# Softmax sums in four 64 x 64 matmuls instead of eight 128 x 32, and a smaller scratch for software DMA

## The chip, the cores and the metric

The kernel runs on one core of a Trainium2 chip. The metric is the device time of one execution in microseconds; lower is better. Of the kernel before, three runs were timed: 1777.71, 1780.35 and 1787.36 us, median 1780.35. One more execution was recorded by the hardware profiler; all durations below are from it.

The core has five engines, each with its own queue of instructions: PE (TensorE, matmuls, and PEld for its weight loads), DVE (VectorE), ACT (ScalarE), POOL (GpSimd) and SP (SyncE, here only a queue that issues DMAs). Sixteen DMA engines move data. A DMA that SP or ACT issues is described by hardware; one that POOL issues is described by software, in a scratch space in SBUF whose size the kernel sets.

## What is computed

`x` has 2048 rows of 1024. The result is `x + A(LN(x)) + B(LN(x))`. B is a dense layer, a tanh-GELU and a dense layer (1024 to 3584 to 1024). A is attention with a recurrent memory: the sequence is cut into 64 segments of 32 rows; each segment attends to itself and to 8 memory rows, and the first 8 rows of its output are the next segment's memory:

```python
mem = mem0                                     # 8 rows
for s in range(n_seg):                         # 64 segments, one after the other
    h = concatenate([mem, xs], axis=1)         # 8 + 32 rows
    q, k, v = h @ Wq, h @ Wk, h @ Wv           # 32 heads of 128
    scores = where(mask, q @ k.T * scale, -1e9)
    p = softmax(scores)
    o = (p @ v) @ Wo
    mem = o[:, :8]
    outs.append(o[:, 8:])
```

Each of the four weights has 1024 x 4096 bf16 values, 8 MB. Together they are 32 MB, more than SBUF holds, so a part has to come from HBM again in each segment.

## The kernel before

It works in two stages. The first (0 to about 400 us) is the layer norm and B, for all rows; its result, with `x` added, goes to HBM as the residual (`res_d`, `resL_d`), and the normalized rows go there turned, ready to be weights (`rows_d`, `rowsL_d`).

The second stage is a loop over the 64 segments, written out in full by Python. A segment has eight half passes (K, Q, V and O, each in halves u = 0 and 1 of 16 heads), and each half pass has eight weight units of 128 x 2048 values (512 KB). In the first six the 32 rows of the segment are the stationary operand, loaded into the array as 128 x 32 column tiles, and the weights stream past: `product` (L830) makes four matmuls of 512 columns for a unit, in the four column tiles of the array, which run side by side. `o_product` (L1089) does the same with the attention's output. Of the 64 units, 47 stay in SBUF and 17 are streamed, 15 of them by SP's DMAs from HBM into a ring of six slots (L284) and two from copies that are kept in PSUM (L273, DVE). A slot is filled again once PE has used it.

Order is written out by hand (`manual_schedule`): steps of the attention are put between the units of a half pass by tables such as `SUMS_0`, `SUMS_1`, `VALUES_0`. For one half u the steps are: `scores` (L947, L953: PE, results in the PSUM bank `mixed`), `exps` (ACT, then a mask by DVE), `sums` (below), and `values` (L1039, L1045: PE, tiles of 64 rows x 128 columns, into two other banks). `sums` occurs 128 times: twice a segment.

In `sums` the exponentials of a half lie on the partitions as four blocks of 32, one for each residue j of the head number; `prA` has 4 x 40 columns, `prB` 4 x 2 x 8. For each block j, a matmul against a column of ones (and zeros elsewhere, `bd[:, j:j+1]`, spread over 32 columns) puts the sum over the block's partitions on all 32 partitions of that block: four matmuls for `prA` (L985, 160 columns) and four for `prB` (L991, 64 columns, added to the same place). ACT turns the sums into reciprocals by Ln and Exp (L996, L999); the Exp is done twice, with a bias `off` that blanks every other head, and DVE multiplies (L1012, L1017, L1024).

Between two segments the first rows of the output go back as memory: DVE adds (L1221), `put_mem` (L320) turns them by a matmul with `ident_mem`, four runs of 8 columns of the identity, and DVE copies them (L330) into `hr_home`, beside the rows of `x` for the next segment. After that, DVE adds the residual to the output (L1243), which PE's next half pass does not need, but which stands on DVE's queue ahead of the K turn (L896, L913) that it does need.

From segment 7 on POOL's queue has, for each segment (`loads`; before that ACT's queue):

- the output of the last segment, four copies of 12 KB (L1276); where i4 = s mod 4 is 1 at the segment that ended, two copies to `outL_d` (L1249) and five from there to the output (L1273) instead
- the next segment's rows, 64 KB (L292), into the half of `hr_home` that the output leaves
- if i4 = 0, `hrL` for the rows that four segments share, 64 KB (L297)
- this segment's residual, 64 KB (L1182), once PE has done with the rows there; if i4 = 1, `resL` too, 64 KB (L1208)
- if i4 = 3, a copy in SBUF (L1191)

In segments 1 to 4 POOL also copies the last residuals within HBM (L523).

The low end of SBUF is laid out by hand: at byte 0 of each partition the scratch for software DMA (`SCRATCH`, 320 bytes), behind it `hr_home`, `qL`, `pd_main` and `ident_mem`, then three slots `low0` to `low2`, up to byte 16384.

Of the kernel before, what the change touches and what calls it, by code (L numbers as in the profile page):

```python
# [10 lines left out]
BF16 = mybir.dt.bfloat16  # L11
U32 = mybir.dt.uint32
F32 = mybir.dt.float32
# [4 lines left out]
P = 128  # L18
# [20 lines left out]
NL = SEG - NX  # L39
# [6 lines left out]
NUNIT = 64  # L46
STREAMED = 17
LOW = 3
SCRATCH = 320
SMALL = 3776  # L50
LEAD = 6
AHEAD = 2
ADD_FIRST = 4
# [67 lines left out]
def kernel(  # L121
# [16 lines left out]
    nc = tc.nc  # L138
# [25 lines left out]
    place = nc.lookup_mloc("DynamicDMAScratchLoc")  # L164
    assert place.addr == 0 and list(place.dims) == [P, SCRATCH + SMALL + LOW * 4096]
    nc.dynamic_dma_scratch_size = SCRATCH
    place.dims = [P, SCRATCH]
    nc.lookup_mls("DynamicDMAScratchLoc").tensor_shape = [P, SCRATCH]
    low = {
        f"low{k}": nc.alloc_sbuf_tensor_at(f"low{k}", [P, 2048], BF16, offset=SCRATCH + SMALL + 4096 * k) for k in range(LOW)  # L170
    }

    hr_home = nc.alloc_sbuf_tensor_at("hr_home", [P, 512], BF16, offset=SCRATCH)[:, :]
    qL = [
# [7 lines left out]

    homes = [hr_home[:, 0:256], hr_home[:, 256:512]]
    small_consts = consts.tile([P, 16], BF16, name="small_consts")
    bd, off = small_consts[:, 0:4], small_consts[:, 4:8].bitcast(F32)

    def slab(place):
        if place in low:
# [3 lines left out]

    ident = homes[1][:, 0:P]
    make_identity(nc, ident)
    ident_mem = nc.alloc_sbuf_tensor_at("ident_mem", [P, 4, NL], BF16, offset=SCRATCH + 3712)[:, :, :]
    nc.vector.tensor_copy(out=ident_mem[:, :, :], in_=ident.rearrange("p (j t) -> p j t", j=4)[:, :, NX:SEG])
    nc.vector.memset(bd[:, :], 0.0)
    nc.vector.memset(off[:, :], NEVER)
    for j in range(4):
        q = slice(32 * j, 32 * j + 32)  # L200
        nc.vector.memset(bd[q, j:j + 1], 1.0)
        nc.vector.memset(off[q, j % 2:j % 2 + 1], 0.0)


# [144 lines left out]
    with tc.tile_pool(name="ma", bufs=2) as ma:  # L349
# [235 lines left out]
        for tg in range(4):  # L585
# [57 lines left out]
            if not last:  # L643
# [7 lines left out]
                for t in range(4):  # L651
# [6 lines left out]
                    for nb in range(2):  # L658
                        cs = slice(nb * 512, (nb + 1) * 512)
                        ps = new_ps()  # L660
                        for fc in range(FC):
                            nc.tensor.matmul(  # L662
                                ps[:, :],
                                lhsT=gts[fc // 4][:, fc % 4, t * P:(t + 1) * P],
                                rhs=w2_sb[fc // 2][:, fc % 2, cs],
                                start=(fc == 0),
                                stop=(fc == FC - 1),
# [68 lines left out]
    with tc.tile_pool(name="late", bufs=1) as late:  # L736
# [66 lines left out]
        for s in range(NSEG):  # L803
# [123 lines left out]
            def ends(t):  # L927

                return t.rearrange("p c (a b) -> p c a b", b=NL)[:, :, ::4, :]
# [50 lines left out]
            def sums(u):  # L980
                prA, prB = st["pr", u]
                dA = mixed[:, 0:160].rearrange("p (c q) -> p c q", q=40)
                for j in range(4):
                    q = slice(32 * j, 32 * j + 32)
                    nc.tensor.matmul(  # L985
                        dA[q, :, :], lhsT=bd[:, j:j + 1].to_broadcast([P, 32]), rhs=prA, start=True, stop=False,
                        skip_group_check=True, tile_position=(0, 32 * j),
                    )
                for j in range(4):
                    q = slice(32 * j, 32 * j + 32)  # L990
                    nc.tensor.matmul(  # L991
                        ends(dA[q, :, :]), lhsT=bd[:, j:j + 1].to_broadcast([P, 32]),
                        rhs=prB,
                        start=False, stop=True, skip_group_check=True, tile_position=(0, 32 * j),
                    )
                nc.scalar.activation(out=mixed[:, 0:160], in_=mixed[:, 0:160], func=ACT.Ln)  # L996

                for b in (1, 0):
                    nc.scalar.activation(  # L999
                        out=mixed[:, 160 * b:160 * b + 160], in_=mixed[:, 0:160], func=ACT.Exp, scale=-1.0,  # L1000
                        bias=off[:, b:b + 1],
                    )
                pdA = pd_main.rearrange("p (c b q) -> p c b q", c=4, b=2)
                if u:
                    pdB = q_all[:, 512:640].rearrange("p (c b a q) -> p c b a q", c=4, b=2, q=NL)
                else:
                    c0 = 0 if first else NL * slot
                    pdB = left_outs[1 if first or i4 >= 2 else 0][:, :, c0:c0 + NL].rearrange(
                        "p (c b a) q -> p c b a q", c=4, b=2
                    )  # L1010
                dd = mixed[:, 0:320].rearrange("p (b c q) -> p b c q", b=2, q=40)
                nc.vector.tensor_tensor(  # L1012
                    out=pdA.rearrange("p c b q -> p b c q"), in0=prA[:, None, :, :].to_broadcast([P, 2, 4, 40]),
                    in1=dd, op=ALU.mult,
                )
                if u:
                    nc.vector.tensor_tensor(  # L1017
                        out=pdB.rearrange("p c b a q -> p b c a q"),
                        in0=prB[:, None, :, :, :].to_broadcast([P, 2, 4, 2, NL]),
                        in1=dd.rearrange("p b c (e q) -> p b c e q", q=NL)[:, :, :, ::4, :], op=ALU.mult,  # L1020
                    )
                else:
                    for a in range(2):
                        nc.vector.tensor_tensor(  # L1024
                            out=pdB[:, :, :, a, :].rearrange("p c b q -> p b c q"),
                            in0=prB[:, None, :, a, :].to_broadcast([P, 2, 4, NL]),
                            in1=dd[:, :, :, 32 * a:32 * a + NL], op=ALU.mult,
                        )
                st["pd", u] = pdA, pdB
# [98 lines left out]
            if left_q[0] and not first:  # L1128
# [6 lines left out]
                0: [lambda: nc.vector.transpose(out=nat_home, in_=nat_home)],  # L1135
            }
            at[4 if first else SUMS_0[i4]] = [lambda: sums(0)] + ([] if first else [lambda: q_left(1)])
            if left_q[1] and not first:
                at[0].insert(0, lambda: keep_q(1))
# [29 lines left out]
            else:  # L1169
                at.setdefault(n0, []).append(lambda: values(0, (0,)))  # L1170
                at.setdefault(n1, []).append(lambda: values(0, (1,)))
            at.setdefault(5 if first else SUMS_1[i4], []).append(lambda: sums(1))

            psV1, psV1L = half_pass("V", 1, left_v[1], at)
# [139 lines left out]
```

## Time and profile before

| | us |
|---|---|
| runs, median (3) | 1780.35 (1777.71 to 1787.36) |
| the profiled execution | 1788.29 |
| its span, first to last instruction | 1786.6 |
| PE busy | 1697.1 (95%) |
| DVE, ACT, POOL busy | 987.9, 670.5, 300.4 |
| mean granted PE clock | 0.998 |
| HBM read, written | 573.43 MB, 28.90 MB |
| L985, first four matmuls of `sums` | x512, 33.2 busy |
| L991, second four | x512, 27.9 busy |

How to read it: a group of instructions is named by its line in the kernel, its engine and operation and its tiles (output, arrow, inputs). Matmuls in different column tiles overlap, so 512 L985 of about 235 ns each make only 33.2 us of busy time; what a step costs PE is read from the starts. A bracket in a timeline is the time that the engine stood idle before the instruction, and what ended it; "issue" there is idle time that nothing in the profile explains. The times "to landing" of a DMA run from its issue to the last byte's arrival.

### The profile page before, as it was taken

How to read it: one execution, taken by the hardware profiler on the slowest of the kernel's cores; microseconds unless marked ns; L12 is line 12 of the kernel's file. 1: busy time of each engine (PE TensorE's matmuls, PEld its weight loads, DVE VectorE, ACT ScalarE, POOL GpSimd, SP SyncE). 2: the span in 40 equal slices, each digit the busy share in tenths (PEclk: the TensorE clock that was granted, in tenths of full speed). 3: DMA queues.
4: the chain of work that ended last, by engine and by line, in shares of the span. 5: the costliest groups of instructions: out<-in, count | busy, mean ns of one | idle time of the engine just before them, and what ended most of it. 6: DMA issues, size and time to landing. Idle time of an engine off the chain costs nothing.

```text
span 1786.6 us, 70503 instructions
## 1 busy us (share of the span) xinstructions
PE 1697.1 (95%) x30600; PEld 867.5 (49%) x30600; DVE 987.9 (55%) x2642; ACT 670.5 (38%) x1709; POOL 300.4 (17%) x586
## 2 busy tenths in 40 slices
PE   9999999998999999999999999999999999999988
PEld 5444444444445544444545444454445445445444
DVE  7657483825555555555555555555555555555544
ACT  6334251603333333333333333343334333333333
POOL 0000002401231111111121211111121111111111
PEclk9999999999999999999999999999999999999999
DMA  9455312779999999999999999999999999999998
GB/s 278 146 167 169 91 45 71 267 277 335 387 390 388 387 374 383 380 383 367 393 378 382 374 381 393 389 388 389 375 387 400 389 389 394 380 378 396 378 376 316
DMA packets 232827, 594.37 MB, mean 333 GB/s; under 512 B 57715, under 2 KB 88035, under 8 KB 232516
## 3 DMA queue, kind: packets, MB, share of 16 engines
q1 hardware_dynamic: 197584, 567.08, 84.3%
q0 software_dynamic: 16896, 16.85, 2.8%
q10 hardware_dynamic: 18036, 5.94, 1.3%
q8 instruction: 239, 3.92, 0.9%
q14 instruction: 72, 0.59, 0.1%
HBM read 573.43 MB, written 28.90 MB: 337 GB/s over the span
## 4 chain that ended last, share of the span: by engine, by line
PE 70%; DMA 18%; DVE 4%; issue 3%; ACT 3%; ACTq 1%; SPq 1%; DVEq 0%
PE acc L830 36%; PE acc L1089 11%; PE ps L534 10%; DMA u<-Wc_O 10%; PE ps L662 6%; DMA u<-Wc_V 5%; PE ps L693 3%; PE acc L1039 1%; ACTq L459 1%; ACT mixed L999 1%; PE mixed L947 1%; SPq L521 1%; DMA hr_home<-res_d 1%; DVE pd_main L1012 1%; PE mixed L320 1%
## 5 line engine op out<-in xcount | busy, mean ns | idle before, releaser
L830 PE MATMUL acc<-u,hr_home 128*32 128x512 bf16 x11520 | 763.6, 380 | 19.7 <-DMA u<-Wc_V 10.2
L830 PEld LDWEIGHTS <-hr_home 128*32 128x32 bf16 x12288 | 337.8, 96 | 303.2 <-issue 45.2
L830 PE MATMUL acc<-u,hrL 128*32 128x512 bf16 x2880 | 253.0, 382 | 4.0 <-DMA hrL<-rowsL_d 2.1
L534 PE MATMUL ps<-u 128*128 128x512 bf16 (+1 forms) x992 | 195.1, 358 | 0.4 <-DMA u<-in_B_w_dram 0.4
L273 DVE TENSOR_SCALAR u<-kept 128x512 uint32<-128x512 uint32 x254 | 163.1, 684 | 48.0 <-PE acc L830 40.6
L1089 PE MATMUL acc<-u,d_oL 128*32 128x512 bf16 x2592 | 170.4, 380 | 13.0 <-issue 10.2
L882 ACT CAST d_oL<-acc 128x512 bf16<-128x512 f32 x143 | 82.0, 584 | 253.9 <-PE acc L830 220.9
L662 PE MATMUL ps<-u 128*128 128x512 bf16 x672 | 146.0, 379 | 0.0
L534 PEld LDWEIGHTS <-u 128*128 128x128 bf16 x992 | 91.6, 98 | 102.1 <-DMA u<-in_B_w_dram 0.6
L1089 PE MATMUL acc<-u,kq 128*32 128x512 bf16 (+1 forms) x2696 | 132.4, 320 | 8.1 <-DMA u<-Wc_O 6.4
L1012 DVE TENSOR_TENSOR pd_main<-kq,mixed 128x320 bf16<-128x320 bf16 x128 | 62.5, 488 | 129.2 <-ACT mixed L999 129.2
L909 ACT CAST kq<-acc 128x256 bf16<-128x256 f32 x256 | 89.4, 375 | 109.7 <-PE acc L830 76.6
L1089 PEld LDWEIGHTS <-kq 128*32 128x32 bf16 x3344 | 87.4, 96 | 84.0 <-ACT kq L1058 24.2
L1276 POOL DMA_DIRECT2D out_dram<-hr_home x168 | 85.4, 516 | 220.5 <-DVE hr_home L1243 220.5
L913 DVE STREAM_TRANSPOSE kq<-kq 128x256 bf16<-128x256 bf16 x256 | 98.2, 422 | 42.8 <-ACT kq L909 42.7
L886 ACT CAST kq<-acc 128x512 bf16<-128x512 f32 x128 | 75.2, 588 | 114.1 <-PE mixed L953 111.7
L977 DVE TENSOR_TENSOR kq<-kq,mixed 128x96 bf16<-128x96 bf16 (+1 forms) x256 | 38.1, 190 | 143.8 <-ACT kq L967 87.2
L830 PEld LDWEIGHTS <-hrL 128*32 128x32 bf16 x3072 | 86.3, 96 | 58.4 <-issue 3.7
L662 PEld LDWEIGHTS <-u 128*128 128x128 bf16 x672 | 65.5, 98 | 78.8 <-DVE u L619 0.4
L611 ACT ACTIVATE u<-ps,b1col 128x512 bf16<-128x512 f32 x112 | 76.5, 684 | 64.5 <-PE ps L534 61.7
L1089 PEld LDWEIGHTS <-d_oL 128*32 128x32 bf16 x2592 | 64.0, 96 | 69.5 <-issue 23.5
L999 ACT ACTIVATE mixed<-mixed,small_consts 128x160 f32<-128x160 f32 x256 | 94.2, 368 | 8.4
(127 smaller groups left out, 1910.5 us busy)
## 6 DMA issues: line engine op xcount, KB each, us to landing
u<-Wc_K SPq DMA_DIRECT2D x256, 512.0 KB
u<-Wc_V SPq DMA_DIRECT2D x256, 512.0 KB
u<-Wc_O SPq DMA_DIRECT2D x256, 512.0 KB
u<-Wc_Q SPq DMA_DIRECT2D x192, 512.0 KB
u<-in_B_w_dram SPq DMA_DIRECT2D x28, 512.0 KB
u<-in_A_Wq_dram SPq DMA_DIRECT2D x13, 512.0 KB
u<-in_A_Wv_dram SPq DMA_DIRECT2D x12, 512.0 KB
u<-in_A_Wk_dram SPq DMA_DIRECT2D x9, 512.0 KB
```

Of the source, the lines that this page charges most:

```text
L273: nc.vector.tensor_single_scalar(out=out, in_=in_, scalar=0, op=ALU.bitwise_or)
L534: nc.tensor.matmul(ps[:, SEG * s0:SEG * s1].rearrange("p (s t) -> p s t", t=SEG), lhsT=w1_sb[fb // 2][:, kt, (fb % 2) * P:(fb % 2 + 1) * P ...
L611: nc.scalar.activation(out=xb[:, :], in_=ps[:, :], func=ACT.Identity, bias=b1col[:, fb:fb + 1], scale=1.0)
L662: nc.tensor.matmul(ps[:, :], lhsT=gts[fc // 4][:, fc % 4, t * P:(t + 1) * P], rhs=w2_sb[fc // 2][:, fc % 2, cs], start=(fc == 0), stop=(fc ...
L830: nc.tensor.matmul(o, lhsT=lhs[:, i, :], rhs=m, start=(i == seq[0]), stop=(i == seq[-1]), tile_position=(0, 32 * j),)
L882: cp(out=out, in_=ps.rearrange("p (h e) -> p h e", e=32))
L909: nc.scalar.copy(out=q_home[:, h0:h1, NL:40], in_=ps[:, 32 * h0:32 * h1].rearrange("p (h e) -> p h e", e=32))
L913: nc.vector.transpose(out=half, in_=half)
L999: nc.scalar.activation(out=mixed[:, 160 * b:160 * b + 160], in_=mixed[:, 0:160], func=ACT.Exp, scale=-1.0, bias=off[:, b:b + 1],)
L1012: nc.vector.tensor_tensor(out=pdA.rearrange("p c b q -> p b c q"), in0=prA[:, None, :, :].to_broadcast([P, 2, 4, 40]), in1=dd, op=ALU.mult,)
L1089: nc.tensor.matmul(acc[r0:r0 + rows, 0:256 * len(blocks)], lhsT=lhsT, skip_group_check=True, rhs=o_columns(t, k, blocks), start=start, sto ...
L1276: loads.dma_start(out=out_flat[rows, 256 * j:256 * j + 256], in_=res[32 * j:32 * j + NX, :])
```

## The change

The ones are kept as `of_head`, 128 x 64: rows of even blocks have ones in columns 0 to 31, rows of odd blocks in columns 32 to 63. A matmul takes 64 partitions (two blocks) at once and gives 64 partitions of sums, so two matmuls do for `prA` and two for `prB`, in the tiles (0, 0) and (64, 64) of the array. `of_head` takes 128 bytes of a partition, where `ident_mem` had 64. To make room the scratch for software DMA shrinks from 320 to 256 bytes, everything between it and `low0` moves down by 64 bytes, and `ident_mem` goes to byte 16384, into unused bytes of the 32-byte cells of small constants, as four runs of 16 bytes, 32 bytes apart. `bd` is gone from `small_consts`.

```diff
-SCRATCH = 320
-SMALL = 3776
+SCRATCH = 256
+SMALL = 3840
...
-    bd, off = small_consts[:, 0:4], small_consts[:, 4:8].bitcast(F32)
+    off = small_consts[:, 0:4].bitcast(F32)
...
-    ident_mem = nc.alloc_sbuf_tensor_at("ident_mem", [P, 4, NL], BF16, offset=SCRATCH + 3712)[:, :, :]
+    ident_mem = nc.alloc_sbuf_tensor_at("ident_mem", [P, 4, 2 * NL], BF16, offset=16384)[:, :, 4:4 + NL]
+    of_head = nc.alloc_sbuf_tensor_at("of_head", [P, 64], BF16, offset=SCRATCH + 3712)[:, :]
...
-    nc.vector.memset(bd[:, :], 0.0)
+    nc.vector.memset(of_head[:, :], 0.0)
...
-        nc.vector.memset(bd[q, j:j + 1], 1.0)
+        nc.vector.memset(of_head[q, 32 * (j % 2):32 * (j % 2) + 32], 1.0)
...
-                for j in range(4):
-                    q = slice(32 * j, 32 * j + 32)
+                for r in range(2):
+                    q = slice(64 * r, 64 * r + 64)
                     nc.tensor.matmul(
-                        dA[q, :, :], lhsT=bd[:, j:j + 1].to_broadcast([P, 32]), rhs=prA, start=True, stop=False,
-                        skip_group_check=True, tile_position=(0, 32 * j),
+                        dA[q, :, :], lhsT=of_head[q, :], rhs=prA[q], start=True, stop=False,
+                        skip_group_check=True, tile_position=(64 * r, 64 * r),
                     )
-                for j in range(4):
-                    q = slice(32 * j, 32 * j + 32)
+                for r in range(2):
+                    q = slice(64 * r, 64 * r + 64)
                     nc.tensor.matmul(
-                        ends(dA[q, :, :]), lhsT=bd[:, j:j + 1].to_broadcast([P, 32]),
-                        rhs=prB,
-                        start=False, stop=True, skip_group_check=True, tile_position=(0, 32 * j),
+                        ends(dA[q, :, :]), lhsT=of_head[q, :], rhs=prB[q],
+                        start=False, stop=True, skip_group_check=True, tile_position=(64 * r, 64 * r),
                     )
```

## The prediction

> **What bounds the kernel now.** I read the page first, then the timeline of PE around one `sums`, then that of POOL, and last the times to landing.
>
> ```profile
> span 1786.6 us, 70503 instructions
> PE 1697.1 (95%) x30600; PEld 867.5 (49%) x30600; DVE 987.9 (55%) x2642; ACT 670.5 (38%) x1709; POOL 300.4 (17%) x586
> ```
>
> PE is busy nearly throughout, so what a step adds to PE's own order of work is on the path. But PE is not alone: in stretches of the segment loop (600 to 684, 1000 to 1085, 1400 to 1486 us) the DMA share is 0.99 to 1.01 at 376 to 390 GB/s, and PE waits there for streamed weights, 20 us in all by name (L830 on `Wc_V` 10.2, on `Wc_O` 9.6). A little more PE time can thus vanish in these waits, not much.
>
> PE from 1000 to 1024 us (start, length, line, shape; matmuls of column tiles run together, so only starts tell):
>
> ```profile
> 1003.86 0.26 PE L985 MATMUL mixed<-kq,small_consts 128*32 128x160 bf16 x4
> ...
> 1010.16 0.39 PE L830 MATMUL acc<-u,hrL 128*32 128x512 bf16 x4
> 1010.49 0.21 PE L1039 MATMUL acc<-pd_main,kq 64*128 64x80 bf16 x1
> 1010.52 0.18 PE L1045 MATMUL acc<-kq,VL 64*128 64x32 bf16 x1
> ...
> 1010.72 0.17 PE L1045 MATMUL acc<-kq,VL 64*128 64x32 bf16 x1
> 1010.82 0.25 PE L985 MATMUL mixed<-kq,small_consts 128*32 128x160 bf16 x4
> 1010.90 0.20 PE L991 MATMUL mixed<-kq,small_consts 128*32 128x64 bf16 x4
> 1010.93 0.39 PE L830 MATMUL acc<-u,hr_home 128*32 128x512 bf16 x4
> ```
>
> Four L830 of 512 columns start every 0.215 us. From 1010.16 to the first matmul of `values` (64 rows) are 0.33 us, so going from 128-row to 64-row tiles costs 0.12. Inside `values` a step is about 0.03; from its last matmul to L985 (128 rows again) it is 0.10, so coming back costs 0.07 to 0.08. The same steps stand in all 128 visits of `values` (medians 0.312 and 0.104). A whole `sums` takes 0.11 here and 0.10 at 1003.86 (to the next L830 at 1003.96). By columns it must take (160 + 64) x 0.215 / 512 = 0.094: the eight matmuls already run at the speed of their columns.
>
> POOL, early and in the loop; brackets give idle time before, and what ended it:
>
> ```profile
> 528.67 1.12 POOL L523 DMA_DIRECT2D res_d<-R_n  x2 [3.64 <-issue]
> 529.79 0.55 POOL L523 DMA_DIRECT2D resL_d<-R_n  x1
> 530.33 0.55 POOL L523 DMA_DIRECT2D res_d<-R_n  x1
> 534.32 0.55 POOL L523 DMA_DIRECT2D resL_d<-R_n  x1 [3.44 <-issue]
> ```
>
> ```profile
> 1027.30 0.57 POOL L292 DMA_DIRECT2D hr_home<-rows_d  x1 [5.41 <-DMA out_dram<-hr_home]
> 1031.47 0.56 POOL L297 DMA_DIRECT2D hrL<-rowsL_d  x1 [3.61 <-PE acc L830]
> 1034.60 0.56 POOL L1182 DMA_DIRECT2D hr_home<-res_d  x1 [2.57 <-PE acc L830]
> 1041.03 2.02 POOL L1276 DMA_DIRECT2D out_dram<-hr_home  x4 [5.88 <-DVE hr_home L1243]
> ```
>
> ```profile
> 1069.72 2.48 POOL L1273 DMA_DIRECT2D out_dram<-outL_d  x5 [4.54 <-DMA outL_d<-hr_home]
> 1072.19 0.57 POOL L292 DMA_DIRECT2D hr_home<-rows_d  x1
> ```
>
> ```profile
> hr_home<-res_d POOLq DMA_DIRECT2D x57, 64.0 KB, 5.4
> hr_home<-rows_d POOLq DMA_DIRECT2D x56, 64.0 KB, 5.6
> hrL<-rowsL_d POOLq DMA_DIRECT2D x13, 64.0 KB, 5.7
> ```
>
> At 530.88 POOL stops with no semaphore to wait for and goes on 5.65 us after the first copy of its group was issued: one landing later. It has run out of room. Count per DMA engine (16) one entry for each 512-byte piece and one to close a transfer: 64 KB is 9, an 8 KB copy (pieces on eight engines) 3. Then 9 + 3 + 3 + 3 = 18 went out at once and 21 did not. In the loop two 64 KB loads are in flight at 1031.47 (18, no stall), and at 1072.19 five copies of 1 or 3 KB an engine (2 each) and a load, 19, no stall. So the room is 19 or 20 entries with 320 bytes. With 256 it is four fifths, 15.2 to 16: one 64 KB load at a time.
>
> **The change, part by part.** In the built programs the order on each engine differs only in these matmuls and memsets.
>
> 1. *Half the matmuls.* 128 visits x 4 matmuls and 4 weight loads go, 1024 rows of PE in all, but the columns stay: 2 x 160 side by side, then 2 x 64. Gain at most 0.098 - 0.094 = 0.004 us a visit, 0.5 us in all. The weight loads (96 ns) run beside matmuls; uncovered, behind a switch, they are part of the 0.12 above.
>
> 2. *64 x 64 tiles between 128-row work.* Each `sums` now enters and leaves 64-row tiles, as `values` does: +0.12 and +0.08, 0.20 us. In 17 of the 128 visits (i4 = 3, and segment 0) `sums` stands right behind `values`, so the way back is only moved: between 0 and 0.2. Sum: 111 x 0.20 = 22 us, plus 17 x 0.1 = 2: 24 us of PE, 0.4 a segment. Bounds: if all of it fills waits for weights, 10 us or so remain (24 less the 20 named, not all in the right place); if the two tiles, which now write one PSUM bank, go one after the other, 0.094 x 128 = 12 more. The trace has no 64-row pair in one bank (those of `values` write two), so I take side by side, as for the four column tiles of `mixed`, and keep 12 for the range.
> The Trainium skill has this as a rule against the change: TensorEngine Tiling (Array Packing), Key Properties, says that a change of tiling mode drains the TensorE, a change of tile alone does not. By that rule the 17 neighbours (64 x 128 to 64 x 64) pay too, which makes 25.6 instead of 24; the trace agrees with the drain at 0.12 and 0.08.
>
> 3. *Room for software DMAs.* A load must now wait for the landing of the one before; behind a waiting L297 on POOL's queue stand L1182, behind that L1208, L1191 and the output copies. Per segment, from L1243 (DVE adds the residual) to the next L1243, with about 7.5 us from the first `out_dram` to L292 (1041.03 to 1048.98, 1019.86 to 1027.30): i4 = 0: 0.3 + 7.5 + 5.6 (rows) + 5.7 (hrL) + 5.4 (res_d) = 24.5. i4 = 1: 0.3 + 7.5 + 5.6 + 5.4 + 5.0 (resL, L1208) = 23.8. i4 = 2: 0.8 + 5.7 (L1249 to L1273) + 5.9 (two of the five copies must land before L292 fits) + 5.6 + 5.4 = 23.4. i4 = 3: 0.3 + 7.5 + 5.6 + 5.4 = 18.8. The segments last 21.1, 22.6, 20.2 and 21.5 us (means between L330s). So three segments in a row fall behind by 3.4 + 1.2 + 3.2 = 7.8, and the fourth makes up 2.7. L1243 late holds DVE, with the K turn queued behind it (L896, L913; DVE idles only 1.3 us between L1243 at 1062.9 and L947, which PE starts as L913 ends); rows late hold L330, hence PE's next pass.
> How much is PE's depends on the landings: with the medians 7.8 less 1.3 harmless; were all twelve landings in the three segments 0.5 us shorter (the shortest res_d took 3.4), 6 less, and nothing is left. I take 0.25 shorter, since a stalled PE eases the DMA engines: 7.8 - 3.0 = 4.8, less 2.0 harmless (between 1.3 and 2.7), less 1.2 that the drains of these segments lengthen them by: 1.6 per four segments, plus 1.6 of drains: 3.2. From segment 7 on POOL makes these loads (before, ACT's queue): 57 / 4 = 14.25 rounds x 3.2 = 46, plus 7 x 0.4 = 3: +48 us. Ends: +10 (nothing of the room, drains half hidden) and (7.8 - 1.3 - 1.2 + 1.6) x 14.25 + 3 = +101.
> The Trainium skill, DMA: Bandwidth & Descriptors, Terms, gives a descriptor 16 bytes and puts the software queue's into rings in SBUF; by that 320 bytes hold 20 and 256 hold 16, an estimate that the 19 to 20 above agree with.
>
> 4. *The rest.* hr_home moves by 64 bytes; weight loads from it (96 ns) run beside matmuls. `ident_mem` is read in runs of 8 with gaps: 158 L320 of 173 to 183 ns; 10% slower would be 3 us, I take 0. The memsets of `of_head` come while DVE waits for x: 0, or 0.5 us if that cover were gone.
>
> Sum, against the profiled execution's 1788.3: 1788.3 + 48 = 1836. That execution lies 7.9 above the median of the runs shown, 1780.35, so for the median 1828.
>
> **Rivals.** A, above: drains and room, 1828, own range 1800 to 1872.
> B, drains only: POOL's stalls come from something other than the scratch's size, or landings shorten enough. +10 to +24: 1790 to 1804. For it: 1182 and 1208 often wait for PE anyway; against: 18 passes and 21 does not, just at 320 bytes.
> C, A with the two tiles one after the other: up to +12, less where POOL sets the pace: 1831 to 1840. Gotcha 1 in the Trainium skill's TensorEngine Tiling (Array Packing) has it that different row tiles cannot use one PSUM bank at once; no run here shows it yet.
> D, hidden: the loop is held by DMA at share 1.0, and 0.4 us a segment disappears in waits for weights, with B's room: 1780 to 1788. Against it: named waits are 20 us, not spread evenly.
> E, faster: the switch costs nothing for 64 x 64 tiles, and PE starts the next L830 in the free half of the array while `sums` streams. A visit could lose its whole 0.098 us: 128 x 0.098 = 12.5, 1768. It decides in E's favour if more than 0.07 us of the 0.098 go (8.9 us, 0.5%). Against: `values` pays for its switch in every one of 128 visits.
>
> **How the numbers follow.** A 0.66, B 0.16, C 0.08, D 0.05, E 0.05. The time is A's, 1828. A change of under 0.5% (8.9 us) is about what cannot be told from none. Slower by more: A + B + C = 0.90; the same: D; faster: E. The range leaves out D, E, B's lowest and A's highest part: 1793 to 1872.
>
> **What would show it.** In the changed kernel's PE timeline the step from L830 to L985 is 0.31 instead of 0.19, from L991 to L830 0.10 instead of 0.03; L985 to L991 stays near 0.07 (C: 0.13). On POOL, L297, L1182 and L1208 show idle time "issue" after the load before, ending at its landing; L1243 waits for DMA far more than 15.2 us in all; L330 and L947 get waits. Wrong if POOL shows none of these (B), or if the steps around L985 are as before (E, D).

## The result, and the profile after

| | before | after |
|---|---|---|
| median, us (6 runs each) | 1782.96 (1777.71 to 1788.56) | 1908.63 (1903.3 to 1914.37) |
| ratio | | 1.0704, 95% interval 1.067 to 1.0738 |
| span of the profiled execution, us | 1786.6 | 1902.5 |
| PE busy, us | 1697.1 | 1744.3 |
| granted PE clock | 0.998 | 0.983 |

The change costs 125.7 us between the medians (115.9 between the two profiled executions, from which all rows below are). The prediction of 1828 (1793 to 1872) had the sign and, as the rows below show, the place, but only little more than a third of the size. The line numbers of the changed kernel from L196 to L994 are one higher than before (L831 is L830 of before, L274 is L273); after that they are the same.

The page's first lines and the chain that ended last, by engine (before: PE 70%, DMA 18%, DVE 4%, issue 3%):

```profile
span 1902.5 us, 69479 instructions
PE 1744.3 (92%) x30088; PEld 854.4 (45%) x30088; DVE 983.3 (52%) x2642; ACT 670.2 (35%) x1709; POOL 301.2 (16%) x586
...
PE 57%; DMA 23%; issue 9%; DVE 6%; ACT 3%; ACTq 1%; SPq 1%; POOL 1%; DVEq 0%; POOLq 0%
```

PE's share falls from 95% to 92%, though it is busy 47 us longer: it waits 154 us in all, 85 before. PE around one `sums` (start, length, line, shape):

```profile
1063.05 1.49 PE L831 MATMUL acc<-u,hr_home 128*32 128x512 bf16 x24
1064.47 0.26 PE L986 MATMUL mixed<-kq,of_head 64*64 64x160 bf16 x2
1064.56 0.19 PE L992 MATMUL mixed<-kq,of_head 64*64 64x64 bf16 x2
1064.68 1.05 PE L831 MATMUL acc<-u,hr_home 128*32 128x512 bf16 x16
```

Worked out from all records (medians): from the last L831 to the first L986 (the first sum) 309 ns (before 192), from the first sum to the next L831 216 ns (98). That is 0.235 us in each of 111 visits. In the 17 visits behind `values` only the way out is longer, by 0.108. Together 28 us of PE.

POOL's queue over one segment and a half:

```profile
1064.88 0.56 POOL L293 DMA_DIRECT2D hr_home<-rows_d  x1 [5.00 <-DMA out_dram<-hr_home]
1070.46 0.57 POOL L298 DMA_DIRECT2D hrL<-rowsL_d  x1 [5.03 <-PE acc L831]
1076.45 0.55 POOL L1182 DMA_DIRECT2D hr_home<-res_d  x1 [5.42 <-PE acc L1089]
1082.98 2.04 POOL L1276 DMA_DIRECT2D out_dram<-hr_home  x4 [5.98 <-DVE hr_home L1243]
1087.65 0.57 POOL L293 DMA_DIRECT2D hr_home<-rows_d  x1 [2.64 <-DMA out_dram<-hr_home]
```

L298 and L1182 start 5.6 and 6.0 us after the load ahead of them, about one landing. The brackets name PE as the last releaser that the profile shows. Comparing each issue with the landing of the load ahead of it shows another releaser: of the 141 loads of 64 KB that POOL issues in the loop, 58 go out before with the one ahead of them still in flight. After, none does, and 68 go out 0.2 to 0.5 us after that landing. The landings themselves are nearly as before (5.4 and 5.6):

```profile
hr_home<-res_d POOLq DMA_DIRECT2D x57, 64.0 KB, 5.5
hr_home<-rows_d POOLq DMA_DIRECT2D x56, 64.0 KB, 5.6
```

The waits that follow, DVE's and PE's (total us, times, longest), first before:

```profile
DVE hr_home L1243 <- DMA hr_home<-res_d: 15.2, 18, 3.4
PE acc L830 <- DVE u L273: 2.1, 2, 1.6
```

After:

```profile
DVE hr_home L1243 <- DMA hr_home<-res_d: 120.7, 32, 6.0
```

```profile
PE acc L831 <- DVE u L274: 70.1, 30, 4.2
PE acc L831 <- DVE hr_home L1243: 23.6, 10, 3.5
PE acc L1089 <- DMA u<-Wc_O: 14.3, 33, 0.9
PE acc L831 <- DMA hrL<-rowsL_d: 6.3, 6, 1.8
```

L274 is the copy of a weight unit kept in PSUM to its stream slot. It stands on DVE's queue right behind L1243. Here is one such place, DVE after and then the same place of a segment before:

```profile
1082.38 0.29 DVE L1243 TENSOR_TENSOR hr_home<-kq,hr_home 128x256 bf16<-128x256 bf16 x1 [4.25 <-DMA hr_home<-res_d]
1082.58 1.28 DVE L274 TENSOR_SCALAR u<-kept 128x512 uint32<-128x512 uint32 x2
```

```profile
1040.35 0.28 DVE L1243 TENSOR_TENSOR hr_home<-kq,hr_home 128x256 bf16<-128x256 bf16 x1
1041.84 1.29 DVE L273 TENSOR_SCALAR u<-kept 128x512 uint32<-128x512 uint32 x2 [1.22 <-PE acc L830]
```

Before, DVE had 1.22 us to spare there: it waited for PE to leave the slot. After, it comes late itself, and PE stands until 1083.92:

```profile
1080.61 0.60 PE L831 MATMUL acc<-u,hr_home 128*32 128x512 bf16 x8
1083.92 0.62 PE L831 MATMUL acc<-u,hr_home 128*32 128x512 bf16 x4 [2.70 <-DVE u L274]
```

And behind such a stall the clock is halved for a while. Stretches (from:to, length, busy us and instructions of PE, PEld, DVE, ACT, POOL, then granted clock, DMA share, GB/s):

```profile
1072.00:1079.90 7.90, 7.33 (x150) 3.69 (x146) 4.02 (x10) 1.94 (x6) 0.55 (x1) 1.00 1.02 396
1079.90:1083.30 3.40, 1.32 (x28) 0.53 (x17) 0.93 (x3) 0.59 (x1) 0.32 (x1) 1.00 0.99 365
1083.30:1086.70 3.40, 2.78 (x28) 1.21 (x31) 1.47 (x5) 0.41 (x2) 1.72 (x4) 0.50 0.61 211
```

The clock's record has 18 such places at half clock, and before two (the idle end of the execution not counted). Summed over the whole record, idle end included, 33 us are missing to full clock (before 5).

By segment, from one L331 to the next (means from segment 8 on, us):

| | i4 = 0 | 1 | 2 | 3 | sum |
|---|---|---|---|---|---|
| before | 20.99 | 22.55 | 20.33 | 21.52 | 85.4 |
| after | 21.19 | 24.80 | 22.47 | 24.58 | 93.0 |

### The profile page after: what moved, and what is told of

It reads as the page before. It is cut to its first block, busy times and chain, and to the rows that moved or that the text cites. A ratio compares the mean times of both kernels' runs of the same rounds, so it can differ in the third digit from the quotient of the medians.

```text
span 1902.5 us, 69479 instructions
## 1 busy us (share of the span) xinstructions
PE 1744.3 (92%) x30088; PEld 854.4 (45%) x30088; DVE 983.3 (52%) x2642; ACT 670.2 (35%) x1709; POOL 301.2 (16%) x586
## 4 chain that ended last, share of the span: by engine, by line
PE 57%; DMA 23%; issue 9%; DVE 6%; ACT 3%; ACTq 1%; SPq 1%; POOL 1%; DVEq 0%; POOLq 0%
PE acc L831 29%; PE ps L535 10%; DMA hr_home<-res_d 8%; DMA u<-Wc_O 7%; PE ps L663 6%; PE acc L1089 5%; DMA pd_main<-resL_d 4%; PE ps L694 3%; DVE u L274 2%; DMA u<-Wc_V 1%; ACT mixed L999 1%; ACTq L460 1%; PE acc L1039 1%; DVE pd_main L1012 1%; DMA out_dram<-hr_home 1%
## 5 line engine op out<-in xcount | busy, mean ns | idle before, releaser
L831 PE MATMUL acc<-u,hr_home 128*32 128x512 bf16 x11520 | 788.3, 390 | 100.0 <-DVE u L274 70.1
L831 PEld LDWEIGHTS <-hr_home 128*32 128x32 bf16 x12288 | 331.4, 98 | 412.9 <-issue 123.9
L831 PE MATMUL acc<-u,hrL 128*32 128x512 bf16 x2880 | 248.2, 381 | 8.7 <-DMA hrL<-rowsL_d 6.3
L274 DVE TENSOR_SCALAR u<-kept 128x512 uint32<-128x512 uint32 x254 | 162.9, 683 | 17.1 <-PE acc L831 16.1
L1012 DVE TENSOR_TENSOR pd_main<-kq,mixed 128x320 bf16<-128x320 bf16 x128 | 62.5, 488 | 138.6 <-ACT mixed L999 123.5
L831 PEld LDWEIGHTS <-hrL 128*32 128x32 bf16 x3072 | 80.3, 96 | 65.7 <-DMA hrL<-rowsL_d 8.3
```

The source lines that it names most:

```text
L274: nc.vector.tensor_single_scalar(out=out, in_=in_, scalar=0, op=ALU.bitwise_or)
L831: nc.tensor.matmul(o, lhsT=lhs[:, i, :], rhs=m, start=(i == seq[0]), stop=(i == seq[-1]), tile_position=(0, 32 * j),)
L1012: nc.vector.tensor_tensor(out=pdA.rearrange("p c b q -> p b c q"), in0=prA[:, None, :, :].to_broadcast([P, 2, 4, 40]), in1=dd, op=ALU.mult,)
```

## The experiments

All ratios are to the kernel before, with its runs beside them on the same chip.

### The two halves of the change, each alone

Room alone (256 bytes, eight matmuls; everything else in SBUF stays at its place, so that 64 bytes lie unused):

```diff
+ROOM = 256
...
-    nc.dynamic_dma_scratch_size = SCRATCH
-    place.dims = [P, SCRATCH]
+    nc.dynamic_dma_scratch_size = ROOM
+    place.dims = [P, ROOM]
...
```

> The kernel before with the scratch for software DMA cut from 320 to 256 bytes and nothing else; the sums stay eight matmuls of 128 x 32. Theory R (the room is nearly all of the loss; 125 us measured, of which about 28 are the steps into and out of the 64-row tiles: 0.235 us in 111 visits and 0.11 in 17): 1855 to 1890 us, 75 to 105 above before; L298 (hrL), L1182 (res_d) and L1208 (resL) wait on POOL with 'issue', each till the load ahead of it has landed; L1243 waits for DMA far above the 18.7 us of before, L274 (the copy of a kept unit behind L1243) ends PE's waits for some 40 to 70 us, and the granted clock is halved in ten or more stretches of 3.4 us. Rival S (the tile switch is the main cause, the waits on POOL follow from PE being late): within 15 us of before, and no such waits. Rival M (neither alone, only both together: each alone is absorbed): 15 to 40 above.

Measured: 1925.77 us, ratio 1.0807 (1.0748 to 1.0867). The room alone costs 141 us, more than the whole change. The waits of PE are those of after (L274 and L1244 here are L273 and L1243 of before):

```profile
PE acc L831 <- DVE u L274: 73.4, 28, 3.8
PE acc L831 <- DVE hr_home L1244: 30.4, 13, 4.0
```

Of 141 loads none overlaps the one ahead; the clock stands at 0.981. Theory R holds (the room is the loss), and its figure was even too low: it left 28 us to the steps.

Matmuls alone (four of 64 x 64, 320 bytes; L991 is edited in the same way, and the ones fill a whole column):

```diff
...
-                for j in range(4):
-                    q = slice(32 * j, 32 * j + 32)
+                for r in range(2):
+                    q = slice(64 * r, 64 * r + 64)
...
-                        dA[q, :, :], lhsT=bd[:, j:j + 1].to_broadcast([P, 32]), rhs=prA, start=True, stop=False,
-                        skip_group_check=True, tile_position=(0, 32 * j),
+                        dA[q, :, :], lhsT=bd[q, 0:1].to_broadcast([64, 64]), rhs=prA[q], start=True, stop=False,
+                        skip_group_check=True, tile_position=(64 * r, 64 * r),
...
```

> The kernel before, scratch 320 bytes, with the four matmuls of 64 x 64 in sums; their ones are one column spread over 64, so each sum runs over two heads (the denominators are those of pairs of heads: that part of the computation is changed, the shapes and positions are those of after). Theory R: +10 to +28 us, 1790 to 1811: 0.235 us for 111 visits and 0.11 for 17, 28 in all, less what vanishes in waits for streamed weights; no waits with 'issue' on POOL beyond those of before, granted clock 0.995 or more. Rival S: +80 or more. Rival D (hidden): within 8 of before.

Measured: 1784.2 us, ratio 1.0004 (0.9978 to 1.003). The steps are there, 309 and 215 ns, and the time is the same: rival D of this expectation. PE, from the page:

```profile
span 1785.4 us, 69459 instructions
PE 1714.5 (96%) x30068; PEld 849.5 (48%) x30088; DVE 987.2 (55%) x2642; ACT 670.7 (38%) x1709; POOL 300.3 (17%) x586
```

PE is busy 17 us longer than before and waits 19 us less (66.7 for 85.3). So the steps came out of time in which PE would have waited; these two sums show 17 to 19 of the 28 us, and where the rest went they do not tell. The largest item that shrinks is "issue" (waits for which the profile shows no releaser), from 32.9 to 10.0.

Another shape, to see what a step depends on: 128 rows x 64 columns, at column positions 0 and 64.

```diff
...
-                        dA[q, :, :], lhsT=bd[:, j:j + 1].to_broadcast([P, 32]), rhs=prA, start=True, stop=False,
-                        skip_group_check=True, tile_position=(0, 32 * j),
+                        dA[q, :, :], lhsT=bd[:, 0:1].to_broadcast([P, 64]), rhs=prA, start=True, stop=False,
+                        skip_group_check=True, tile_position=(0, 64 * r),
...
```

> The kernel before, scratch 320 bytes, with four matmuls in sums of 128 rows x 64 columns at column positions 0 and 64, ones a single column spread over 64 (every sum runs over all 128 partitions: that part of the computation is changed). It asks whether any change of tile shape costs the step, or only one of the rows. If any change of shape costs it: L830 to the first L985 0.30 us instead of 0.19, last L991 to L830 0.10 to 0.12 instead of 0.02, +10 to +28 us. If only a change of the rows: the steps are those of before and the time is within 8 us of before; L985's two tiles of 160 columns take no longer than four did.

Measured: 1786.21 us, ratio 1.002 (0.9994 to 1.0046).

```profile
999.70 0.84 PE L830 MATMUL acc<-u,hr_home 128*32 128x512 bf16 x12
1000.47 0.26 PE L985 MATMUL mixed<-kq,small_consts 128*64 128x160 bf16 x2
1000.57 0.20 PE L991 MATMUL mixed<-kq,small_consts 128*64 128x64 bf16 x2
1000.69 2.77 PE L830 MATMUL acc<-u,hr_home 128*32 128x512 bf16 x48
```

The steps are 309 and 219 ns, as with 64 rows: it is not the rows, a change from 32 to 64 columns costs the same. And from the last L985 to the first L991 it takes 89 ns here, where both tiles hold all rows, as in the 64 x 64 tiles, where two row tiles write one PSUM bank: those two ran no more one after the other than these do (in both, the two L985 of a pair start 3 ns apart). The expectation's time of +10 or more for this case failed for the same reason as in the run before.

### Where the 28 us of steps went

The kernel before, and the one with four 64 x 64 matmuls and 320 bytes; in both, 5 of the 15 units that SP streams in a segment are not loaded from segment 8 on (PE uses what the slot holds; the second has the edit of the matmuls alone besides):

```diff
+CUT = [unit for unit in ORDER if IS_STREAMED[unit] and unit not in KEPT][1::3]
...
-        unit, t = streams[n], slab(slot)
+        unit = streams[n]
+        if n >= 8 * STREAMED and unit in CUT and slot in last_in:
+            stream_tiles[n], slot_of[n] = last_in[slot], slot
+            return
+        t = last_in[slot] = slab(slot)
```

> The kernel before, where from segment 8 on 5 of the 15 units that SP streams in each segment are not loaded: PE multiplies with what the slot still holds (so the products of these units are wrong: 147 of 573 MB of reads are left out). It is the base for the next run. PE is idle for 85 us in the kernel before, 11 on Wc_V, 10 on Wc_O and 33 with 'issue'. Theory D (in the loop the streamed weights set the pace, PE time of up to 28 us is hidden behind them): PE's idle time for weights and 'issue' goes, 20 to 60 us faster, 1720 to 1765. Rival: PE sets the pace already, within 15 us of before.

> The same 5 units not loaded, with the four 64 x 64 matmuls in sums (ones as a column over two heads, scratch 320 bytes). Theory D (the steps into and out of the tiles, 0.235 us in 111 visits and 0.11 in 17, 28 us, cost nothing with all the streams only since they lie in waits for weights): with fewer streams they come out, 18 to 30 us above the run with eight matmuls and fewer streams. Rival H (they are hidden in waits for DVE or ACT, or PE makes them up otherwise): within 8 us of it, whatever the streams.

Measured: eight matmuls 1733.81 us, ratio 0.9749 (0.9717 to 0.978); four 1748.52, ratio 0.983 (0.9799 to 0.9862). The stretch from 1000 to 1085 us, eight and then four (before: DMA share 1.00):

```profile
1000.00:1085.00 85.00, 82.85 (x1891) 44.28 (x1887) 48.04 (x132) 34.73 (x98) 16.42 (x31) 1.00 0.83 274
```

```profile
1000.00:1085.00 85.00, 83.37 (x1806) 42.10 (x1802) 47.58 (x131) 32.38 (x92) 17.65 (x34) 1.00 0.82 269
```

With DMA to spare, the steps cost 14.7 us; with all streams, nothing. So the loop before is paced by the streamed weights (45 us go with a third of them), and that hides about half of the steps. The 14.7 lie between the two theories, nearer to D's 18: about 13 us are hidden even here. Of these some 8 can be named, as H's: PE's waits fall from 51 to 43 us, those for DVE's multiplication (L1012 of before) from 8.0 to 4.2 and those with "issue" from 6.0 to 2.8.

### The room, from the other side

First, who makes POOL's lateness PE's. The add L1243 on POOL instead of DVE, so that L274 need not stand behind it:

```diff
-                nc.vector.tensor_tensor(out=to, in0=o, in1=r_rows, op=ALU.add)
+                (nc.vector if left_o or s < EARLY_SEGS else nc.gpsimd).tensor_tensor(out=to, in0=o, in1=r_rows, op=ALU.add)
```

> The changed kernel with the residual add L1243 given to POOL (where s is 7 or more and i4 is not 1) instead of DVE; the scratch stays 256 bytes and the sums stay four matmuls. Theory Q (what makes POOL's lateness PE's is that DVE stands in L1243 till res_d lands, with the copy L274 of a kept weight unit behind it): POOL's waits with 'issue' stay, PE's waits for L274 fall from 70 us to under 25 (those of segments with i4 = 1, which still add on DVE, remain), and 30 to 80 of the 125 us come back: 1830 to 1880. Rival T (the chain on POOL itself, landing after landing, is longer than a segment and sets the pace whoever adds): the rows of the next segment (L293) come late instead, L331 waits for them, and the time is within 20 of after, 1890 to 1930; an add on POOL would then lengthen the chain by its own duration in 43 segments.

Measured: 1894.49 us, ratio 1.0629 (1.059 to 1.0668), about 14 us below after; theory Q had 30 to 80.

```profile
PE acc L831 <- DVE hr_home L1243: 58.7, 13, 6.6
PE acc L831 <- DMA hrL<-rowsL_d: 16.9, 11, 3.0
```

PE's waits for L274 are gone, as theory Q has it, but the time is T's: other waits take their place, 58.7 us for the adds that stay on DVE (i4 = 1, where the residual `resL_d` now lands up to 7.8 us late) and 16.9 for `hrL`. T's own sign (L331 waiting for the rows) did not come. DVE's queue is the way on which the delay reaches PE; the delay is POOL's line of loads.

So take loads out of that line. The residual from ACT's queue, the room still 256 bytes:

```diff
-            loads.dma_start(out=homes[s % 2], in_=res_d[s + 1, :, :])
+            nc.scalar.dma_start(out=homes[s % 2], in_=res_d[s + 1, :, :])
```

> The changed kernel with one DMA moved: the load of the residual (L1182, 64 KB) is issued from ACT's queue in every segment, instead of POOL's from segment 7 on. Scratch 256 bytes, sums in four matmuls. Theory R (what costs is that POOL's queue can hold one 64 KB load at a time, so that its loads stand in line, landing after landing): without res_d the lines on POOL are 0.3 + 7.5 + 5.6 + 5.7 = 19.1 us at i4 = 0, 18.4 at 1 and 18.0 at 2, each below its segment of 20.3 to 22.6, so nearly all comes back: 1780 to 1815 us; L1243's waits for res_d fall from 120.7 us to under 25. Rival U (with 256 bytes every software DMA is slower, or the outputs' copies are what is late): 40 us or more above before remain, 1825 or more, with L331 waiting for the rows.

Measured: 1805.07 us, ratio 1.0148 (1.0107 to 1.0189). One moved DMA brings back about 100 of the 126 us. DVE's waits in L1243 for `res_d` are 18.3 us, the clock 0.996. What stays is one thing:

```profile
PE acc L831 <- DMA hrL<-rowsL_d: 21.3, 14, 2.7
```

```profile
1205.20 0.56 POOL L293 DMA_DIRECT2D hr_home<-rows_d  x1 [5.26 <-DMA out_dram<-hr_home]
1211.55 0.56 POOL L298 DMA_DIRECT2D hrL<-rowsL_d  x1 [5.79 <-PE acc L831]
```

In all 13 segments L298 goes out 0.35 us after the rows have landed, and 3.2 to 5.8 us after the start of PE's last use of the buffer. Before, it goes out 0.87 us after that start, with the rows still 1.1 to 2.8 us from landing. There PE's next use comes 6.7 to 7.6 us after the issue; 5.7 us to land leave 1 to 2 us. The prediction had this load in POOL's line, but not PE's own wait for it.

Both loads from ACT's queue:

```diff
-                load_left_rows(g + 1, loads)
+                load_left_rows(g + 1, nc.scalar)
...
-            loads.dma_start(out=homes[s % 2], in_=res_d[s + 1, :, :])
+            nc.scalar.dma_start(out=homes[s % 2], in_=res_d[s + 1, :, :])
```

> The changed kernel with the residual (L1182) and the rows that four segments share (L298) both loaded from ACT's queue; scratch 256 bytes, four matmuls. With the residual alone moved, 27 us of the loss were left, and L298 was issued 0.35 us after the rows' landing in all 13 segments, PE then waiting 21.3 us for hrL. Theory R (only the room for 64 KB loads in POOL's queue): L298 is issued under 1 us after PE's last use, PE's waits for hrL fall to under 4 us, 1775 to 1795 us, within 1% of before. Rival W (something else of the change, the layout or ident_mem in gaps, costs too): 1800 or more stay.

Measured: 1788.57 us, ratio 1.0022 (1.0 to 1.0043). PE's waits, from the longest:

```profile
PE acc L1089 <- DMA u<-Wc_O: 10.9, 26, 1.1
PE mixed L321 <- DVE kq L1221: 6.2, 26, 1.0
PE acc L831 <- DMA u<-Wc_V: 5.9, 12, 1.6
```

With four matmuls, 256 bytes and the new layout all in place, two DMAs on another queue undo the loss. So nothing else of the change (`ident_mem` in gaps, the move of `hr_home`) costs more than the interval's 0.4%.

Is there something to win in this line before? The residual from ACT with 320 bytes, and 384 bytes of room:

```diff
-            loads.dma_start(out=homes[s % 2], in_=res_d[s + 1, :, :])
+            nc.scalar.dma_start(out=homes[s % 2], in_=res_d[s + 1, :, :])
```

> The kernel before with the same one DMA moved to ACT's queue (scratch 320 bytes, eight matmuls). DVE's L1243 waits 15.2 us for res_d in the kernel before; POOL's waits with 'issue' in the loop are 14 us. If those are on the path: 5 to 15 us faster, 1765 to 1780. If the streamed weights set the loop's pace (DMA share 0.99 to 1.01): within 8 us of before, although the waits of L1243 go to nearly none. If the issue on ACT (0.33 us) in front of ACT's copies hurts: 56 x 0.33 = 18 us slower at most.

```diff
-SCRATCH = 320
-SMALL = 3776
+SCRATCH = 384
+SMALL = 3712
...
-    ident_mem = nc.alloc_sbuf_tensor_at("ident_mem", [P, 4, NL], BF16, offset=SCRATCH + 3712)[:, :, :]
+    ident_mem = nc.alloc_sbuf_tensor_at("ident_mem", [P, 4, 2 * NL], BF16, offset=16384)[:, :, 4:4 + NL]
```

> The kernel before with 384 bytes of scratch instead of 320 (the 64 bytes are had by putting ident_mem into the gaps of the constants, as the change does); eight matmuls. Theory: 320 bytes hold two 64 KB loads, which is all that the loop asks for; POOL's waits with 'issue' in the loop (14 us) go, but the streamed weights set the pace: within 8 us of before. The early copies L523, 27 us of waits with 'issue' at 320 bytes, should wait less (24 entries instead of 19 or 20). If the room at 320 costs still: 8 to 20 us faster.

Measured: 1783.68 us, ratio 1.0019 (0.9989 to 1.0048), and 1784.74, ratio 1.0007 (0.9984 to 1.0029). Neither wins anything. In the first, L1243 waits for `res_d` even longer (35.4 us in 37 places, the longest 2.1), and PE does not feel it: about 1 us at a time DVE can take. In the second the early copies L523 wait 44.8 us with "issue":

```profile
  issue: 44.8, 18
```

They wait 59.5 us with 320 bytes (not 27, as the expectation had it) and 73.1 with 256. The room acts there too, in the same order, but nothing waits for these copies.

### Both halves together, once more

The changed kernel at 256 bytes (1.0704) lay below eight matmuls at 256 bytes (1.0807). Both kinds in before's layout, on one chip, each with the edits of the two halves above:

> The kernel before with 256 bytes of scratch and eight matmuls once more, beside the next run on one chip. Before it measured 1.081 of before, the changed kernel 1.070 on another occasion. If the difference is of the kernels: 1.075 to 1.087 again. If it was of the occasions: 1.066 to 1.074.

> The kernel before with 256 bytes of scratch and the four 64 x 64 matmuls (ones as a column over two heads: the denominators are those of pairs), all else as before. Theory P (with POOL's line of loads setting the pace, the steps of the tiles cost nothing; PE only waits less): not above the run with eight matmuls and 256 bytes by more than 8 us. If the four matmuls even win back time there (the changed kernel lay some 15 us below the eight at 256 bytes): 5 to 20 below it, and if that was the layout, the same as it. If the steps add to the line of loads: 15 to 28 above it.

Measured: eight 1924.3 us, ratio 1.0787 (1.0745 to 1.083); four 1912.51, ratio 1.073 (1.0683 to 1.0777). So the layout is not the reason, and the steps add nothing to the line of loads (theory P). Whether four matmuls win 12 us there is not settled, since the intervals overlap; with the two earlier runs it looks so. One difference in the profiles is the clock: 57 us are missing to full clock with eight, 33 with four; but the same eight missed only 37 in the first of their two profiles, so this does not settle it. Another is the landings of the residual: 5.6 and 5.8 us on the mean in the two profiles with eight, 5.4 and 5.5 in those with four. Whether that is a cause was not tested.

## Why the prediction was wrong

- *The room for software DMAs.* The count was right: 18 entries pass at 320 bytes, and at 256 one 64 KB load at a time, 58 overlaps turned into none. The lines on POOL came out nearly as worked out: from one L1243 to the next 24.7, 24.4 and 23.7 us at i4 = 0, 1 and 2 (means from segment 8 on), for 24.5, 23.8 and 23.4. With each segment's excess reaching PE in the next one (L1243 stands at its start), 3.4, 1.2 and 3.2 were expected at i4 = 1, 2 and 3, and +2.25, +2.14 and +3.06 were measured, stalls, halved clock and steps together.
- *The step that failed is the choice behind "I take 0.25 shorter" and "less 2.0 harmless".* In all, four segments lose 7.6 us (93.0 less 85.4), where the sum had 3.2; in 14.25 rounds that is 108 of the 116 us between the profiled executions. The first choice took 3.0 off the 7.8 us per four segments. It had a reason (a stalled PE eases the DMA engines) but no row, and the three lines above came out 1.1 us longer in their sum than worked out, not 3.0 shorter.

  The second choice looked at the K turn. But first on DVE's queue behind L1243 stands, in each of the 56 segments from segment 8 on, the kept copy L273, and before the change DVE is idle ahead of it for only 0.9, 1.1, 0.2 and 0.9 us at i4 = 0 to 3 (means). Such slack also counts only once, since an L1243 that uses it up starts POOL's next line that much later. An estimate from these rows: PE loses 3.4 - 1.1 = 2.3, then 1.1 + 1.2 - 0.2 = 2.1, then 0.2 + 3.2 - 0.9 = 2.5 us, close to the three measured; of the 7.8 only the last 0.9 is harmless.

  The prediction's own lower bound of 1.3 for the harmless part, with the landings' medians, leaves 6.5, and with its drains gives its upper end of +101. The number was in the text, put at the end of the range.
- *The clock was left out.* A PE stall such as the 2.7 us above halved the clock afterwards, and 29 us more than before are missing to full clock (33 less 5, from unrounded values). No term of the sum had that. About half of it lies in the segments with i4 = 3, the ones that lost more than the estimate above (3.06 for 2.5), so it probably lifts the time past +101; how much of the 29 lies under waits and costs nothing was not measured apart.
- *The drains* (the steps into and out of the 64-row tiles). 24 us of PE were predicted; 28 are in the trace, in the places named (0.31 for L831 to L986 was right; L992 to L831 is 0.12 instead of 0.10). But at 320 bytes they cost nothing that can be measured (1.0004, 0.9978 to 1.003), and at 256 bytes nothing either. Their mechanism was rival D's, at 0.05: waits of PE swallow them. What spoke against D was a count of waits by name, 20 us. It left out 33 us of waits with "issue", of which 23 went when the steps came.
The Trainium skill, TensorEngine Tiling (Array Packing), Key Properties, has a drain at each change of tiling mode. The trace agrees, with 0.12 us on the way in and 0.10 to 0.12 on the way out, for 64-row tiles and for 128 x 64 ones, and for the way out of the 17 neighbours of `values` as well (+0.108 each).
- *Rival C* (two row tiles in one PSUM bank go one after the other) is out: 89 ns for both shapes. *B* is out by the room alone, *E* by the first trace.
- *Half the matmuls:* no gain shows, as predicted.

## What to carry to other kernels

When a change takes bytes from the scratch of software DMA, list which software transfers are in flight together and what each one adds; if two that used to overlap no longer fit, every instruction behind the second on that queue moves by a whole landing, and one transfer moved to another queue can be worth more than the bytes. A PE cost is worth only what PE's waits of that stage leave of it, and waits without a named releaser belong in that count. Where a bound in the rows and a hopeful adjustment without a row differ, take the bound. And slack that a late instruction has used up is not there again for the next one of the same line.

## What the runs showed that was not expected

- In these traces the granted clock changes only on a fixed grid of 3.413 us, and PE need not be idle for the whole of a stretch. In the changed kernel (600 to 1700 us), each of the 13 stretches with under 1.48 us of PE busy was followed by one at half clock. Of the 308 with more, one was, and that one was itself at half clock; in other profiles the border lies between 1.3 and 1.7. PE's ends are modelled, so the border is rough. A stall of 2.7 us was enough (1081.2 to 1083.9 above).
The Trainium skill, TensorE: Matmul & The Clock Gate, Why this matters for your kernels, advises against idle gaps above about 3 us, one idle window being enough to halve the clock. One stretch of the grid was enough here too; the gap that suffices is shorter, 2.7 us.
- Going from 128 x 32 to 128 x 64 column tiles costs as much as going to 64-row tiles (309 ns to the first sum against 192).
- A bracket that names PE can hide a full software queue: L298's wait (residual on ACT's queue) was put down to PE in 12 of the 13 segments, and it was issued 0.35 us after a landing in every one.
